# Experts' first layer: a set's four sums kept in PSUM banks instead of SBUF tiles

## The chip, the cores and the metric

One Trainium2 (trn2) chip, one core. The metric is the device time of one execution in microseconds (us). A program's time is the median of its runs.

## What is computed

Three stages follow each other: a causal attention with a decay (4 batches, 8 heads, 576 positions, head size 64), a layer `h*cos(h)` between two matrix products, and the stage that the change touches, a mixture of eight experts over 2304 tokens whose gates come from eight Sinkhorn rounds:

```python
def _moe2_ref(x, w_gate, w1, w2):
    N, D = x.shape                       # 2304, 512
    E = w_gate.shape[1]                  # 8
    logits = x @ w_gate
    logits = logits - logits.max()
    P = np.exp(logits)
    for _ in range(8):
        P /= P.sum(1, keepdims=True) + 1e-09
        P /= P.sum(0, keepdims=True) + 1e-09
        P *= N / E
    out = np.zeros((N, D), dtype=np.float32)
    for e in range(E):
        h = np.maximum(x @ w1[e], 0.0)   # w1[e]: 512 x 1024
        ye = h @ w2[e]                   # w2[e]: 1024 x 512
        out += P[:, e:e + 1] * ye
    return out
```

## The kernel before, in words

The experts run as 48 **blocks**: three groups of 768 tokens (`p`), eight experts (`e`), and two halves of an expert's 1024 hidden units (`hb`). A block has a first layer and a second layer. fp32 operands are held as two fp16 numbers, a high and a low part, and a product of two such operands is three matmuls (`PASSES`).

**First layer** (`first_layer`, called twice a block, for two **sets** `m` of 256 hidden units). A set is a 2x2 block product of 256 hidden units by 768 tokens, done with seven products in place of eight (`PRODUCTS`, products 0 to 6). Each product is six matmuls of 128x384 (`product`, L1203) into a PSUM bank. Products 0, 2, 4 and 6 accumulate in one bank `y`; product 1 has a bank `b` of kind `bq`; products 3 and 5 accumulate in a second bank `q` of kind `bq`. Between products the bank is read while it still grows. From these readings come four sums: c11 (from product 1 and the copy p1 of `y`), c22 (from `y` after product 4 and the copy p5 of `q`), c12 (from `q` after product 5 and the copy u2 of `y`) and c21 (`y` after product 6). A copy is ScalarE's (`copy`, L1230), an addition VectorE's (`add`, L1235), and each writes an SBUF tile `ct` of a ring of twelve. ScalarE then makes the high part of the rectified sum (`relu_split`, L1222, SBUF to SBUF), and VectorE its low part as `max(sum, 0) - high` (L1223). The low part's instruction is called **low** below; it is not issued at once but put in the list `lows` and taken from it by `low()` at fixed places of the order.

```python
            product(p, w, 4, y, False)
            c22 = add(y, p5)
            relu_split(m, 1, 1, c22)
            hook()
            product(p, w, 5, q, False)
            c12 = add(q, u2)
            ...
            product(p, w, 6, y, False)
```

Product 6 writes the bank `y` from which c22 is read, so it waits until VectorE's addition c22 is done. VectorE works its instructions in the order of the program; in a set that order is: c11, low of c11, c22, c12, low of c22, low of c12, and the low of c21 in the next set or at the second layer's start.

**Second layer** (`second_layer`): 72 matmuls of 128x512 (L1279) into banks of kind `a`, six token tiles of 128; VectorE adds each, times its gate, to `acc` (L1308).

**PSUM** has eight banks: three of kind `a`, three of kind `bq`, two of kind `y`. A kind's banks are given out in turn, and a bank is written anew when its last reader is done. Before, a set takes two `bq` banks.

**The weights of the next block** are made while a block runs: ScalarE scales them (L1046) and makes high parts (L1055), GpSimd (POOL) makes the weight sums (L1016 to L1019) and all low parts (L1066, 256 elements at a time, SBUF to SBUF). They are handed out by a plan over the groups of the second layer, but POOL's share runs on into the next first layer: the last of it, `wb`, is eight instructions in a row.

**The gates** (`sinkhorn`) are worked during the first three blocks, a step at a time: `hook()` is called seven times a set and twelve times a second layer, 26 times a block, and at listed counts takes one step. A step's matmul uses a `bq` bank.

Of the kernel before, what the change touches and what calls it, by code (L numbers as in the profile page):

```python
# [23 lines left out]
def kernel(  # L24
# [18 lines left out]
    KD = DM // P  # L43
# [12 lines left out]
    NCH = len(CH)  # L56
# [99 lines left out]
    def at(where, n, fn):  # L156
        where.setdefault(n, []).append(fn)
# [48 lines left out]
    with tc.manual_schedule():  # L206
# [556 lines left out]
        largest = keep.tile([P, KD * NCH], F32, name="largest")  # L763
# [15 lines left out]
        def find_scale(nm, cols, bank):  # L779

            gm, gr, scale, back = small["gm"], small["gr"], scales[nm], backs[nm]
            nc.vector.tensor_reduce(gm, cols, axis=AX.X, op=ALU.max)
            yield
            ps = bank()
            nc.tensor.transpose(ps[0:1, 0:P], gm, ident)
            nc.vector.tensor_reduce(gr[0:1, 0:1], ps[0:1, 0:P], axis=AX.X, op=ALU.max)
            yield
            ps = bank()
            nc.tensor.matmul(ps[:, 0:1], ones[0:1, :], gr[0:1, 0:1], start=True, stop=True)
            nc.vector.tensor_scalar(back, ps[:, 0:1], 2.0**-LIMIT, 2.0**LIMIT, ALU.max, ALU.min)  # L790
            nc.vector.tensor_scalar(back.bitcast(I32), back.bitcast(I32), 0x7F800000, None, ALU.bitwise_and)
            nc.vector.tensor_scalar(
                scale.bitcast(I32), back.bitcast(I32), -1.0, float((254 + TOP) << 23), ALU.mult, ALU.add
            )
            nc.vector.tensor_scalar(back, back, 2.0**-TOP, None, ALU.mult)
            yield
# [46 lines left out]
        def split_x(j, xt):  # L843
            c0, n = CH[j]
            for x in range(KD):
                a = acc[:, x, c0 : c0 + n]
                nc.scalar.copy(xt[:, 0, x, :], a)
                nc.vector.tensor_tensor(xt[:, 1, x, :], a, f32(xt[:, 0, x, :]), ALU.subtract)
                nc.vector.tensor_reduce(
                    largest[:, KD * j + x : KD * j + x + 1], a, axis=AX.X, op=ALU.max, apply_absolute_value=True  # L850
                )
                yield
# [4 lines left out]
        def logits(j, xt, step, bank):  # L857
            n = CH[j][1]
            ps = bank()
            for kk in range(KD):  # L860
                for s in range(2):
                    nc.tensor.matmul(
                        ps[:, 0:n], wg_of[0][:, kk, :], xt[:, s, kk, :], start=kk + s == 0, stop=kk == KD - 1 and s == 1
                    )
            lg = keep.tile([P, 512], F32, tag="dm", name="lg")
            nc.scalar.copy(lg[0:16, 0:n], ps[0:16, 0:n])
            if step is not None:
                at(after_l2, step, lambda: logits2(j, lg, bank))
            return lg

        def logits2(j, lg, bank):
            c0, n = CH[j]
            ps = bank()
            nt = n // P
            for x in range(nt):
                nc.tensor.matmul(
                    ps[:, x * NE : (x + 1) * NE], lg[0:16, x * P : (x + 1) * P], sel, start=True, stop=True
                )
            nc.vector.tensor_copy(
                gate[:, c0 // P : c0 // P + nt, :], ps[:, 0 : nt * NE].rearrange("p (t e) -> p t e", e=NE)  # L880
            )
# [30 lines left out]
        for n in range(len(items) + LAG):  # L912
            if n < len(items):
                ps = ahead.pop(n) if n in ahead else layer1(*items[n])
            for fn in after_l1.pop(n, []):
                fn()
            if n >= LAG:
                b, j, i = items[n - LAG]
# [19 lines left out]
        HN = 384  # L938
# [19 lines left out]
        ctmp = []  # L958
# [13 lines left out]
        XL = xp.tile([P, 2, KD, CH[-1][1]], F32R, name="xl")  # L972
        turn_of = {"ct": 0, "tm": 0, "sg": 0}

        def take(kind, tiles):
            n = turn_of[kind]
            turn_of[kind] = n + 1
            return tiles[n % len(tiles)]
# [155 lines left out]
        def bank(kind, bufs):  # L1134
            return ps_e.tile([P, 512], F32, tag=kind, name=kind, bufs=bufs)


        def rows():
            rs = small["rs"]
            nc.vector.tensor_reduce(rs, gate, axis=AX.X, op=ALU.add)  # L1140
            nc.vector.tensor_scalar(rs, rs, 1e-9, None, ALU.add)
            nc.vector.reciprocal(rs, rs)
            nc.vector.tensor_tensor(gate, gate, rs[:, :, None].to_broadcast([P, NT // P, NE]), ALU.mult)
            nc.vector.tensor_reduce(small["cs"], gate.rearrange("p t e -> p e t"), axis=AX.X, op=ALU.add)

        def sinkhorn():
            yield from split_x(NCH - 1, XL)
            lg = logits(NCH - 1, XL, None, lambda: bank("bq", 3))
            yield
            logits2(NCH - 1, lg, lambda: bank("bq", 3))  # L1150
            nc.vector.tensor_reduce(small["gm"], gate, axis=AX.XY, op=ALU.max)
            yield
            ps = bank("bq", 3)
            nc.tensor.transpose(ps[0:1, 0:P], small["gm"], ident)
            nc.vector.tensor_reduce(small["gr"][0:1, 0:1], ps[0:1, 0:P], axis=AX.X, op=ALU.max, negate=True)
            yield
            ps = bank("bq", 3)
            nc.tensor.matmul(ps[:, 0:1], ones[0:1, :], small["gr"][0:1, 0:1], start=True, stop=True)
            nc.vector.tensor_copy(small["ngm"], ps[:, 0:1])
            nc.scalar.activation(gate, gate, AF.Exp, bias=small["ngm"])  # L1160
            rows()
            yield
            finding = find_scale("x1", largest[:, 2 * KD :], lambda: bank("bq", 3))
            for it in range(8):
                ps = bank("bq", 3)
                nc.tensor.matmul(ps[:, 0:NE], ones, small["cs"], start=True, stop=True)
                cf = small["cf"]
                nc.vector.tensor_scalar(cf, ps[:, 0:NE], 1e-9, None, ALU.add)
                nc.vector.reciprocal(cf, cf)
                nc.vector.scalar_tensor_tensor(  # L1170
                    gate, gate, float(NT) / NE, cf[:, None, :].to_broadcast([P, NT // P, NE]), ALU.mult, ALU.mult
                )
                if it + 1 < 8:
                    rows()
                    next(finding, None)
                else:

                    undo = small["gr"]
                    nc.vector.scalar_tensor_tensor(undo, backs["w1"], 1.0 / RAISE, backs["w2"], ALU.mult, ALU.mult)
                    for p, nm in enumerate(("x0", "x1", "x1")):  # L1180
                        g = gate[:, p * TT : (p + 1) * TT, :]
                        nc.vector.tensor_scalar(g, g, undo, backs[nm], ALU.mult, ALU.mult)
                    gates_ready.append(True)
                yield

        gates_ready = []
        sink = sinkhorn()

        GATE_STEPS = (1, 2, 3, 4, 6, 9, 15, 18, 21, 24, 29, 36, 41, 45, 49, 55, 58)
        slot = [0]  # L1190

        def hook():
            slot[0] += 1
# [31 lines left out]
        def first_layer(p, m):  # L1225
            w = W1T[m]

            def copy(ps):
                c = take("ct", ctmp)
                nc.scalar.activation(c, ps[:, 0:HN], AF.Copy, scale=RAISE)  # L1230
                return c

            def add(ps, other):
                c = take("ct", ctmp)
                nc.vector.scalar_tensor_tensor(c, ps[:, 0:HN], RAISE, other, ALU.mult, ALU.add)  # L1235
                return c

            y = bank("y", 2)
            product(p, w, 0, y, True)
            p1 = copy(y)  # L1240
            hook()
            low()
            b = bank("bq", 3)
            product(p, w, 1, b, True)
            c11 = add(b, p1)
            hook()
            low()
            product(p, w, 2, y, False)
            u2 = copy(y)
            relu_split(m, 0, 0, c11)  # L1250
            hook()
            low()
            q = bank("bq", 3)
            product(p, w, 3, q, True)
            p5 = copy(q)
            hook()
            product(p, w, 4, y, False)
            c22 = add(y, p5)
            relu_split(m, 1, 1, c22)
            hook()  # L1260
            product(p, w, 5, q, False)
            c12 = add(q, u2)
            relu_split(m, 0, 1, c12)
            hook()
            low()
            product(p, w, 6, y, False)
            c21 = copy(y)
            relu_split(m, 1, 0, c21)
            hook()
            low()  # L1270
# [123 lines left out]
```

## Time and profile before

| | |
|---|---|
| median of three runs | 2147.79 us (2146.71 to 2150.45) |
| profiled execution, its time | 2150.18 us |
| its span, first to last instruction | 2148.4 us |
| mean granted TensorE clock | 0.998 |
| busy: ScalarE 63%, POOL 60%, VectorE 58% of the span | |
| share of the chain that ended last: PE 78%, VectorE 10%, ScalarE 5%, issue 4% | |

The profiled execution's own time is 1.8 us more than its span and 2.4 us above the median of the runs. The experts' blocks begin at 670 us and fill the rest. PE is TensorE, DVE VectorE, ACT ScalarE. A matmul's duration overlaps with that of the next one, so a row of six matmuls of 326 ns each takes about 0.97 us from its start to the next product's start.

### The profile page before, as it was taken

To read this page: it belongs to the slowest core of one execution; us is meant where nothing else is said; L and a number is where in the kernel's file an instruction comes from. 1 tells how busy PE (TensorE), PEld (TensorE's weight loads), DVE (VectorE), ACT (ScalarE), POOL (GpSimd) and SP (SyncE) were. 2 spreads that over 40 slices of the span, in tenths; PEclk is the share of its full clock that TensorE was granted. 3 is DMA by queue.
4 is the path that set the end of the run, shared out by engine and by line. 5 is a ranking of instruction groups with operands and counts; after the bars stand their busy time and mean duration, and the time that the engine had idled before them with its cause. 6 is when DMAs were issued, how large, how long until landed. Compare 5 with 4: busy or idle time off the path is not lost.

```text
span 2148.4 us, 34045 instructions
## 1 busy us (share of the span) xinstructions
PE 2061.7 (96%) x12461; PEld 1298.2 (60%) x12461; DVE 1245.3 (58%) x2250; ACT 1351.1 (63%) x2479; POOL 1285.5 (60%) x1794
## 2 busy tenths in 40 slices
PE   8999999999999999999999999999999999999998
PEld 7888988888876544454455444544454445444544
DVE  8999778685656754444455444444555444444444
ACT  7888787777555576555666556556566565556553
POOL 6777455150526576567677675566577755675563
PEclk9999999999999999999999999999999999999999
DMA  5444245353201221122123212221123212212221
GB/s 127 101 106 112 75 163 179 121 177 103 75 1 60 79 75 57 66 79 71 58 69 108 79 60 69 69 79 59 61 78 108 63 66 69 79 59 68 70 79 30
DMA packets 176919, 177.52 MB, mean 83 GB/s; under 512 B 64752, under 2 KB 131696, under 8 KB 176752
## 3 DMA queue, kind: packets, MB, share of 16 engines
q1 hardware_dynamic: 176752, 175.35, 27.1%
q8 instruction: 98, 1.61, 0.3%
q14 instruction: 69, 0.57, 0.1%
HBM read 165.54 MB, written 4.87 MB: 79 GB/s over the span
## 4 chain that ended last, share of the span: by engine, by line
PE 78%; DVE 10%; ACT 5%; issue 4%; POOL 1%; DMA 1%; SPq 0%; POOLq 0%; ACTq 0%; DVEq 0%
PE a L1279 35%; PE y L1203 16%; PE bq L1203 9%; PE ph L175 4%; PE a L822 4%; PE pv L593 2%; PE pst L543 2%; DVE h L1223 2%; PE pss L486 1%; PE pss L487 1%; PE pv L573 1%; DVE ct L1235 1%; PE psq L366 1%; DVE t L196 1%; DVE dm L135 1%
## 5 line engine op out<-in xcount | busy, mean ns | idle before, releaser
L1279 PE MATMUL a<-wb,h 128*128 128x512 f16 x3456 | 754.9, 379 | 0.2 <-ACT acc L1297 0.2
L1203 PEld LDWEIGHTS <-wa 128*128 128x128 f16 x4032 | 394.4, 98 | 332.6 <-issue 69.9
L1279 PEld LDWEIGHTS <-h 128*128 128x128 f16 x3456 | 338.1, 98 | 401.5 <-issue 0.5
L1203 PE MATMUL y<-xc,wa 128*128 128x384 f16 x2304 | 430.9, 327 | 58.1 <-DVE ct L1235 57.9
L1308 DVE SCALAR_TENSOR_TENSOR acc<-a,gate,acc 128x512 f32<-128x512 f32 x264 | 197.4, 750 | 384.9 <-PE a L1279 384.6
L1223 DVE SCALAR_TENSOR_TENSOR h<-ct,h 128x384 f16<-128x384 f32 x384 | 307.1, 811 | 175.8 <-ACT h L1222 164.2
L1016 POOL TENSOR_TENSOR tm<-sg 128x256 f32<-128x256 f32 x96 | 71.2, 742 | 501.7 <-issue 485.8
L1203 PE MATMUL bq<-xc,wa 128*128 128x384 f16 x1728 | 327.9, 326 | 0.7 <-ACT ct L1230 0.7
L1222 ACT ACTIVATE h<-ct 128x384 f16<-128x384 f32 x384 | 197.9, 522 | 204.3 <-DVE ct L1235 201.3
L1230 ACT ACTIVATE ct<-y 128x384 f32<-128x384 f32 x288 | 140.4, 488 | 279.6 <-PE y L1203 279.5
L1066 POOL TENSOR_TENSOR wb<-sg,wb 128x256 f16<-128x256 f32 x384 | 252.4, 697 | 0.0
L1066 POOL TENSOR_TENSOR wa<-tm,wa 128x256 f16<-128x256 f32 x384 | 250.2, 684 | 0.0
L822 PE MATMUL a<-H,w 128*128 128x512 f32 (+1 forms) x960 | 214.3, 371 | 6.0 <-DVE acc L837 3.0
L175 PE MATMUL ph<-xt,w 128*128 128x512 f32 (+1 forms) x960 | 211.6, 369 | 0.9 <-DVE H L203 0.9
L1046 ACT ACTIVATE sg<-sg,sw 128x1024 f32<-128x1024 f32 x188 | 210.1, 1141 | 0.0
L822 PEld LDWEIGHTS a<-H,w 128*128 128x128 f32 x960 | 175.6, 189 | 32.6 <-ACT H L201 2.9
L175 PEld LDWEIGHTS ph<-xt,w 128*128 128x128 f32 x960 | 174.9, 188 | 24.0 <-DVE H L203 1.2
L1066 POOL TENSOR_TENSOR wa<-sg,wa 128x256 f16<-128x256 f32 x288 | 189.3, 686 | 0.0
L1235 DVE SCALAR_TENSOR_TENSOR ct<-bq,ct 128x384 f32<-128x384 f32 x192 | 106.4, 554 | 93.6 <-PE bq L1203 93.4
L1055 ACT CAST wa<-tm 128x1024 f16<-128x1024 f32 x94 | 98.4, 1047 | 97.0 <-POOL tm L1019 97.0
L128 POOL TENSOR_SCALAR w<-dx 128x512 fp32r<-128x512 f32 x32 | 19.9, 622 | 154.0 <-DVE dx L127 149.3
L1055 ACT CAST wb<-sg 128x512 f16<-128x512 f32 x188 | 107.2, 618 | 3.0
(203 smaller groups left out, 2515.5 us busy)
## 6 DMA issues: line engine op xcount, KB each, us to landing
sg<-in_moe_w_dram SPq DMA_DIRECT2D x192, 512.0 KB
seen<-in_moe_w_dram SPq DMA_DIRECT2D x64, 256.0 KB
u<-in_moe_w_dram SPq DMA_DIRECT2D x64, 256.0 KB
stg<-in_moe_w_in_dram SPq DMA_DIRECT2D x16, 512.0 KB
stg<-in_moe_w_out_dram SPq DMA_DIRECT2D x16, 512.0 KB
q<-q SPq DMA_DIRECT2D x30, 160.0 KB
out_dram<-acc SPq DMA_DIRECT2D x18, 256.0 KB
qr<-in_q_dram SPq DMA_DIRECT2D x32, 128.0 KB
```

The costliest lines, as they stand in the source:

```text
L175: nc.tensor.matmul(ps[:, 0:n], w[:, ws, kk * P : (kk + 1) * P], XT[j][:, xs, kk, :], start=first, stop=kk == KD - 1 and (ws, xs) == PASSES ...
L822: nc.tensor.matmul(a_of[b, j][x][:, 0:n], w[:, s1, DM + x * P : DM + (x + 1) * P], H[:, s2, 0:n], start=i == 0 and n_ == 0, stop=end and n ...
L1046: nc.scalar.activation(t, t, AF.Copy, scale=scale)
L1055: nc.scalar.copy(hi, src)
L1066: nc.gpsimd.tensor_tensor(lo[:, y : y + k, z : z + c], src[:, y : y + k, z : z + c], hi[:, y : y + k, z : z + c], ALU.subtract,)
L1203: nc.tensor.matmul(ps[:, 0:HN], w[:, ws, a, k, :], XCS[p % 2][b][:, xs, k, :], start=fresh and n == 0, stop=n == 5, skip_group_check=not f ...
L1222: nc.scalar.activation(hi, src, AF.Relu)
L1223: lows.append(lambda: nc.vector.scalar_tensor_tensor(lo, src, 0.0, hi, ALU.max, ALU.subtract))
L1230: nc.scalar.activation(c, ps[:, 0:HN], AF.Copy, scale=RAISE)
L1235: nc.vector.scalar_tensor_tensor(c, ps[:, 0:HN], RAISE, other, ALU.mult, ALU.add)
L1279: nc.tensor.matmul(ps, H[:, s1, c * P : (c + 1) * P], W2T[e * NHB + hb & 1][:, 2 * m + z, s2, :], start=start and n == 0, stop=stop and n ...
L1308: nc.vector.scalar_tensor_tensor(a, v, g, a, ALU.mult, ALU.add)
```

## The change

The sums stay in PSUM. c11 is written over product 1's bank `b`, c12 over `q`, c21 over `y` (ScalarE copies the bank onto itself with the scale), and c22 goes from `y` to a third `bq` bank, taken for it. High parts and lows read the sum there. p1, u2 and p5 still go to SBUF tiles. A set now takes three `bq` banks, that is all of them. Since the `bq` banks are so used, a gate step that falls into a first layer (the first 14 of a block's 26 counts) takes a bank of kind `a`, and one in a second layer a `bq` bank as before.

```diff
+        def spare():
+            return bank("a" if (slot[0] - 1) % 26 < 14 else "bq", 3)
...
-                ps = bank("bq", 3)
+                ps = spare()
...
-            def copy(ps):
-                c = take("ct", ctmp)
+            def copy(ps, c=None):
+                c = take("ct", ctmp) if c is None else c[:, 0:HN]
                 nc.scalar.activation(c, ps[:, 0:HN], AF.Copy, scale=RAISE)
                 return c
 
-            def add(ps, other):
-                c = take("ct", ctmp)
+            def add(ps, other, c):
+                c = c[:, 0:HN]
                 nc.vector.scalar_tensor_tensor(c, ps[:, 0:HN], RAISE, other, ALU.mult, ALU.add)
                 return c
...
-            c11 = add(b, p1)
+            c11 = add(b, p1, b)
...
-            c22 = add(y, p5)
+            c22 = add(y, p5, bank("bq", 3))
...
-            c12 = add(q, u2)
+            c12 = add(q, u2, q)
...
-            c21 = copy(y)
+            c21 = copy(y, y)
```

No instruction is added, removed or moved on any engine; operands and waits differ. In the changed file the lines are L1208 (products), L1227 (high part), L1228 (low), L1236 (copy), L1241 (addition).

VectorE, the first five instructions of a first layer late in the program (`ct` are SBUF tiles, `bq` and `y` PSUM banks, `h` the high and low parts in SBUF), before:

```order
L1235 SCALAR_TENSOR_TENSOR ct7_8756<-bq_15849,ct6_8755 128x384 [waits PE_49,Activation_49]
L1223 SCALAR_TENSOR_TENSOR h000_8726<-ct7_8756,h000_8726 128x384 [waits Activation_49]
L1235 SCALAR_TENSOR_TENSOR ct10_8759<-y_15841,ct9_8758 128x384 [waits PE_49,Activation_49]
L1235 SCALAR_TENSOR_TENSOR ct11_8760<-bq_15866,ct8_8757 128x384 [waits PE_49]
L1223 SCALAR_TENSOR_TENSOR h011_8729<-ct10_8759,h011_8729 128x384 [waits Activation_49]
```

and with the change:

```order
L1241 SCALAR_TENSOR_TENSOR bq_15903<-bq_15903,ct6_8755 128x384 [waits DVE_49,PE_49,Activation_49]
L1228 SCALAR_TENSOR_TENSOR h000_8726<-bq_15903,h000_8726 128x384 [waits Activation_49]
L1241 SCALAR_TENSOR_TENSOR bq_15934<-y_15895,ct8_8757 128x384 [waits DVE_49,PE_49,Activation_49]
L1241 SCALAR_TENSOR_TENSOR bq_15920<-bq_15920,ct7_8756 128x384 [waits PE_49]
L1228 SCALAR_TENSOR_TENSOR h011_8729<-bq_15934,h011_8729 128x384 [waits Activation_49]
```

The order stays. The low (second row) had two SBUF operands and now has one in PSUM and one in SBUF; c11 and c22 have a third wait, on VectorE itself, for the earlier low that read the bank they write.

TensorE, the last of product 2 and the start of product 3 in a block's second set, before:

```order
L1203 MATMUL y_17959<-xc02_8719,wa1_8749 128x384
L1203 LDWEIGHTS wa1_8749
L1203 MATMUL y_17959<-xc02_8719,wa1_8749 128x384
L1203 LDWEIGHTS wa1_8749
L1203 MATMUL bq_17985<-xc03_8720,wa1_8749 128x384
```

and with the change:

```order
L1208 MATMUL y_17268<-xc02_8719,wa1_8749 128x384
L1208 LDWEIGHTS wa1_8749
L1208 MATMUL y_17268<-xc02_8719,wa1_8749 128x384
L1208 LDWEIGHTS wa1_8749
L1208 MATMUL bq_17294<-xc03_8720,wa1_8749 128x384 [waits DVE_49]
```

Product 3 of the second set now waits for VectorE: its bank is the one in which the first set's c12 lay, until that sum's low has read it.

## Rows read from the trace of the kernel before

**Rows 1.** The page's first part: busy us (share of the span) xinstructions.

```profile
PE 2061.7 (96%) x12461; PEld 1298.2 (60%) x12461; DVE 1245.3 (58%) x2250; ACT 1351.1 (63%) x2479; POOL 1285.5 (60%) x1794
```

**Rows 2.** Waits of the whole span: who waited for whom, us in total, times, longest.

```profile
PE y L1203 <- DVE ct L1235: 57.9, 40, 2.5
```

**Rows 3.** Timeline of one block's TensorE, 1514 to 1548 us: start, duration, instruction [idle before].

```profile
1533.83 1.14 PE L1203 MATMUL y<-xc,wa 128*128 128x384 f16 x6
1534.81 1.14 PE L1203 MATMUL bq<-xc,wa 128*128 128x384 f16 x6
1537.40 2.11 PE L1203 MATMUL y<-xc,wa 128*128 128x384 f16 x12 [1.45 <-DVE ct L1235]
...
1541.29 1.14 PE L1203 MATMUL bq<-xc,wa 128*128 128x384 f16 x6
...
1544.22 1.14 PE L1203 MATMUL y<-xc,wa 128*128 128x384 f16 x6
```

**Rows 4.** The same stretch on VectorE.

```profile
1532.16 0.56 DVE L1235 SCALAR_TENSOR_TENSOR ct<-bq,ct 128x384 f32<-128x384 f32 x1 [1.28 <-PE bq L1203]
1533.99 2.88 DVE L1223 SCALAR_TENSOR_TENSOR h<-ct,h 128x384 f16<-128x384 f32 x1 [1.27 <-ACT h L1222]
1536.80 0.54 DVE L1235 SCALAR_TENSOR_TENSOR ct<-y,ct 128x384 f32<-128x384 f32 x1
...
1537.93 1.03 DVE L1223 SCALAR_TENSOR_TENSOR h<-ct,h 128x384 f16<-128x384 f32 x2
...
1543.51 0.56 DVE L1235 SCALAR_TENSOR_TENSOR ct<-y,ct 128x384 f32<-128x384 f32 x1 [0.53 <-PE y L1203]
```

**Rows 5.** The same stretch on POOL.

```profile
1531.39 5.07 POOL L1066 TENSOR_TENSOR wb<-sg,wb 128x256 f16<-128x256 f32 x8
```

**Rows 6.** By source line, whole span: duration ns min/median/max, first and last start us.

```profile
L1223 DVE SCALAR_TENSOR_TENSOR h<-ct,h x384: 542/559/3973, 676.5 to 2129.7; 128x384 f16<-128x384 f32 x192
L1235 DVE SCALAR_TENSOR_TENSOR ct<-bq,ct x192: 541/558/559, 673.6 to 2127.6; 128x384 f32<-128x384 f32 x192
L1308 DVE SCALAR_TENSOR_TENSOR acc<-a,gate,acc x264: 735/751/753, 757.5 to 2144.1; 128x512 f32<-128x512 f32 x132
```

**Rows 7.** Timeline of another block, 1076 to 1092 us, three engines.

```profile
1077.15 6.02 POOL L1066 TENSOR_TENSOR wb<-sg,wb 128x256 f16<-128x256 f32 x8
...
1078.12 0.74 DVE L1223 SCALAR_TENSOR_TENSOR h<-ct,h 128x384 f16<-128x384 f32 x1 [1.27 <-ACT h L1222]
...
1080.16 2.11 PE L1203 MATMUL y<-xc,wa 128*128 128x384 f16 x12
```

**Rows 8.** The chain that ended last, 660 to 2148 us: second layers' starts and lengths.

```profile
752.26 15.54 PE a L1279 x72
...
1088.12 15.54 PE a L1279 x72
...
1175.69 15.54 PE a L1279 x72
...
1632.93 15.54 PE a L1279 x72
...
1666.49 15.54 PE a L1279 x72
...
2128.56 15.55 PE a L1279 x72
```

**Rows 9.** Window: us, busy us (x) of PE, PEld, DVE, ACT, POOL, then PEclk.

```profile
1656.80:1660.40 3.60, 3.54 (x12) 1.70 (x12) 1.85 (x5) 2.00 (x4) 0.00 (x0) 0.53 1.06 292
```

**Rows 10.** Groups by form, VectorE, 0 to 670 us: busy us, mean ns of one.

```profile
L563 DVE SCALAR_TENSOR_TENSOR A<-pst,A 128x384 f16<-128x384 f32 x64 | 35.6, 556 | 4.3 <-ACT A L555 2.4
...
L200 DVE TENSOR_TENSOR ph<-ph,t 128x384 f32<-128x384 f32 x32 | 18.0, 562 | 6.4 <-ACT t L197 6.3
```

**Rows 11.** Groups by form, ScalarE, 0 to 670 us: busy us, mean ns of one.

```profile
L193 ACT ACTIVATE u<-ph,quarter 128x384 f32<-128x384 f32 x32 | 18.1, 565 | 4.8 <-PE ph L175 4.8
```

**Rows 12.** TensorE's waits in the first three blocks, 666 to 752 us.

```profile
PE y L1203 <- DVE ct L1235: 3.0, 3, 1.3
```

More of the change, by code (lines that the diff above doesn't have):

```diff
@@ L1135, in bank @@
             return ps_e.tile([P, 512], F32, tag=kind, name=kind, bufs=bufs)
+        gates_ready = []
+        slot = [0]
         def rows():
@@ L1144, in rows @@
             nc.vector.tensor_reduce(small["cs"], gate.rearrange("p t e -> p e t"), axis=AX.X, op=ALU.add)
+        def spare():
+            return bank("a" if (slot[0] - 1) % 26 < 14 else "bq", 3)
         def sinkhorn():
             yield from split_x(NCH - 1, XL)
-            lg = logits(NCH - 1, XL, None, lambda: bank("bq", 3))
+            lg = logits(NCH - 1, XL, None, spare)
             yield
-            logits2(NCH - 1, lg, lambda: bank("bq", 3))
+            logits2(NCH - 1, lg, spare)
             nc.vector.tensor_reduce(small["gm"], gate, axis=AX.XY, op=ALU.max)
             yield
-            ps = bank("bq", 3)
+            ps = spare()
             nc.tensor.transpose(ps[0:1, 0:P], small["gm"], ident)
@@ L1156, in sinkhorn @@
             yield
-            ps = bank("bq", 3)
+            ps = spare()
             nc.tensor.matmul(ps[:, 0:1], ones[0:1, :], small["gr"][0:1, 0:1], start=True, stop=True)
@@ L1162, in sinkhorn @@
             yield
-            finding = find_scale("x1", largest[:, 2 * KD :], lambda: bank("bq", 3))
+            finding = find_scale("x1", largest[:, 2 * KD :], spare)
             for it in range(8):
-                ps = bank("bq", 3)
+                ps = spare()
                 nc.tensor.matmul(ps[:, 0:NE], ones, small["cs"], start=True, stop=True)
@@ L1184, in sinkhorn @@
                 yield
-        gates_ready = []
         sink = sinkhorn()
         GATE_STEPS = (1, 2, 3, 4, 6, 9, 15, 18, 21, 24, 29, 36, 41, 45, 49, 55, 58)
-        slot = [0]
         def hook():
```

## The prediction

> **What bounds the kernel.** TensorE is busy for 96% of the span [rows 1], so first the 4% is to be found. The table of waits gives one large entry on it: 57.9 us, in 40 pieces, in which a product into `y` waits for VectorE's addition [rows 2]. That is product 6 waiting for c22. The timeline of one block shows it: product 4 starts at 1533.83, product 5 at 1534.81, and product 6, which would follow 0.97 us later at about 1535.78, starts at 1537.40 [rows 3]. On VectorE c22 starts only at 1536.80, since the low of c11 in front of it runs from 1533.99 to 1536.87, 2.88 us [rows 4]. The same instruction takes 0.56 us by its median; its longest is 3.97 [rows 6].
>
> Why is it long? On POOL the eight `wb` instructions run from 1531.39 to 1536.46 [rows 5], and the low ends 0.41 us after the last of them. In the experts' blocks 37 lows are like it (36 of 2.9 us, one of 3.97), and each ends 0.41 to 0.42 us after such a run. The low has both operands in SBUF, as have POOL's. Other VectorE instructions run through the same stretches at their usual length: c11's addition at 1532.16, inside the `wb` run, took 0.56 [rows 4, 5]. No addition L1235 takes over 0.559, and no L1308 over 0.753 of a median 0.751, though most of those fall into POOL's runs [rows 6]. Both have one operand in PSUM and one in SBUF. So what a row of POOL instructions holds up is a VectorE instruction with two SBUF operands.
>
> It does not always hold it through the run. In the block at 1078 us the low got in between two POOL instructions and took 0.74, the `wb` run became 6.02 us long in place of 5.07, and product 6 started at 1080.16 almost in step [rows 5, 7].
>
> The chain that ended last gives what this costs a block, as the distance between second layers' starts. From 1088.12 to 1175.69 lie three blocks of this undisturbed kind: 29.19 us each. From 1666.49 to 2128.56 lie 15 held ones: 30.80 each. Of the 45 distances from 752.26 to 2128.56, 36 are near 30.80, eight between 29.19 and 29.44, and one, from 1632.93 to 1666.49, is 33.56 [rows 8]. In that last one the low held longest, TensorE waited 2.5 us [rows 2], and the granted clock then stood at 0.53 for 3.6 us, which is the lower level, 1.2 GHz [rows 9].
>
> **The change, part by part.**
>
> *The low reads its sum in PSUM.* It then has the operands of L1235: PSUM, SBUF, output to SBUF. The nearest row with its very types, 128x384, fp16 from PSUM fp32 and an SBUF fp16, is L563 with 556 ns [rows 10]. So 0.56 us, held or not. In the block of rows 3 the low would end at 1534.55, before product 4 is done, and c22 would start with the end of product 4, as in the second set, where it starts at 1543.51 and product 6 follows at 1544.22 without idle time [rows 3, 4]. Every distance becomes 29.19: 1376.30 - 45 x 29.19 = 62.75 us less [rows 8]. The slow clock of the one block goes with its wait and is in that sum. In what follows nothing else holds the lows back, since c22's, c12's and c21's lows change in the same way.
>
> *c22 goes to a PSUM bank.* This is the one place where little room is left. In the second set c22 ends at 1543.51 + 0.56 = 1544.07, product 6 starts at 1544.22 [rows 3, 4], and in the held block TensorE starts 0.06 after c22's end (1536.80 + 0.54 to 1537.40): 0.09 us of room. No row shows VectorE reading one bank and writing another; below, L1235 with its 558 ns median writes SBUF [rows 6], above, L200 reads and writes PSUM in 562 [rows 10]. I take 562, 0.01 more, and nothing on the path. The added wait on VectorE itself names a low of the set before, long done. What exceeds the room would cost 96 sets x the excess: 0.1 us a set is 9.6 us.
>
> *c21 stays in `y`.* ScalarE reads and writes PSUM; the nearest row for that is L193, 565 ns [rows 11], with the low's 0.56 after the high part. All three together are under 2 us, and the second layer needs c21's parts only in its fourth group, 18 of 72 matmuls after its start, 18/72 x 15.54 = 3.9 us [rows 8]. Nothing.
>
> *Three `bq` banks a set.* The one new wait on TensorE is product 3 of the second set, for the low of c12 of the first. In the held block the lows of c22 and c12 ended at 1537.93 + 1.03 = 1538.96 and that product started at 1541.29 [rows 3, 4]: 2.3 us of room, and the lows now come sooner. Nothing.
>
> *The gates' banks.* Seventeen steps in the first three blocks; their waits go with VectorE's gate work, not with a bank. TensorE's three waits there, 3.0 us together [rows 12], stay.
>
> **Sum.** 62.75 us less against the profiled execution, whose span of 2148.4 becomes 2085.7 and whose own time 2150.18 becomes 2087.4. The median of the runs is 2.39 below that execution: 2147.79 - 62.8 = **2085.0**.
>
> **A rule that speaks against it.** The Trainium skill, page "SBUF — State Buffer", section "Who interferes with whom", says that a VectorE instruction with two SBUF inputs and a GpSimd instruction that reads SBUF exclude each other, and that the second one waits until the first finishes. By that a low would wait for one POOL instruction, as at 1078 us, and not for four, as at 1533.99; the trace shows both, and the long kind 37 times. The same section says that an instruction with at most one SBUF input does not contend, with which L1235 and L1308 agree.
>
> **The rivals.**
>
> *The low stays long.* If a POOL instruction can hold a low for 0.64 us at most (5.07 / 8 [rows 5]), the low would end by 1533.99 + 0.64 + 0.56 = 1535.19, c22 by 1535.75, and product 6 would never wait. The 2.88 us must then have another cause, which the change may leave alone, or the operand that stays in SBUF is enough to be held. This is the case in which the change doesn't do what it says: 2147.8. Against it stand 37 ends at the same distance from POOL's, and 288 additions with one SBUF operand of which none is long. Chance 0.05.
>
> *Part of it comes back as a short wait in every set.* If c22 takes 0.1 to 0.3 us more than its room, 96 sets cost 10 to 29 us: 2095 to 2114. For it speaks the room of 0.09; against it the 562 of L200. Chance 0.05.
>
> *Slower.* The same place, priced higher: VectorE's reading of one bank and writing of another, or its way past an extra wait, takes so long that product 6 waits in all 96 sets and not in 37. It decides from 62.8 / 96 = 0.65 us over the room, that is from a c22 of 0.56 + 0.09 + 0.65 = 1.3 us; at 1.5 us the time would be 2085 + 96 x 0.85 = 2167. No row with a PSUM operand comes near. Chance 0.03.
>
> **How the numbers follow.** The forecast has what is left, 0.87, with a range of its own from 2080 to 2092: below, if the first three blocks' 3.0 us go too and the distance comes down by some hundredths; above, if c22 exceeds its room by some hundredths in each set. The range reaches to the nearer half of the second rival, 2080 to 2099. Within 0.2%, about 4 us, is what a measurement of this kernel can't tell from no change. Faster: 0.87 and the second rival's 0.05, 0.92; same: 0.05; slower: 0.03.
>
> **What would show it.** The low L1228 never over about 0.6 us while POOL's `wb` run passes over it; VectorE's busy time for the 384 lows near 384 x 0.56 = 215 us; the wait of `y` for VectorE down from 57.9 to about 3 us, all of it in the first three blocks; second layers 29.2 apart throughout; no low clock. Wrong would be: lows still ending 0.41 after POOL, or a short wait before product 6 in every set, or one before product 3 of the second sets.

## The result and the profile after

The change makes the kernel faster: 2086.78 us, median of four runs (2085.18 to 2087.94), against 2149.12 for the kernel before in the same comparison (four runs, 2146.71 to 2151.0). The ratio is 0.9717, 95% interval 0.9702 to 0.9732. The profiled span fell from 2148.4 to 2086.1 us and the granted clock stands at 0.999. The predicted 2085.0 us is 1.8 below the median. Of that, 0.5 lies in the sum, which gave 2087.4 us for the profiled execution where 2087.94 was measured. The rest, 1.2, is how the executions happened to fall: the profiled one lay 2.4 us above its median before and lies 1.2 above it now.

The page of the kernel after, its first part (busy us, share of the span, instructions; compare [rows 1]) and the shares of its chain by engine:

```profile
PE 2054.4 (98%) x12461; PEld 1298.1 (62%) x12461; DVE 1156.7 (55%) x2250; ACT 1337.5 (64%) x2479; POOL 1277.8 (61%) x1794
...
PE 90%; DVE 6%; ACT 2%; issue 1%; POOL 1%; DMA 0%; SPq 0%; POOLq 0%; ACTq 0%; DVEq 0%
```

As many instructions as before on every engine, and VectorE is busy for 1245.3 - 1156.7 = 88.6 us less. In the chain TensorE's share went from 78% to 90%.

The lows of the kernel after, by source line (duration in ns min/median/max, first and last start in us):

```profile
L1228 DVE SCALAR_TENSOR_TENSOR h<-bq,h x288: 545/558/560, 676.8 to 2066.4; 128x384 f16<-128x384 f32 x144
L1228 DVE SCALAR_TENSOR_TENSOR h<-y,h x96: 557/558/559, 681.3 to 2067.3; 128x384 f16<-128x384 f32 x96
```

The longest of 384 lows is 560 ns, where it was 3973 [rows 6]. POOL's work has not moved out of their way: 68 of the lows start inside a POOL run, as in the block that [rows 3 to 5] showed. The same block of the kernel after, timeline of TensorE, VectorE and POOL (start, duration, instruction [idle before]):

```profile
1501.46 1.14 PE L1208 MATMUL y<-xc,wa 128*128 128x384 f16 x6
1502.44 1.14 PE L1208 MATMUL bq<-xc,wa 128*128 128x384 f16 x6
1503.41 2.11 PE L1208 MATMUL y<-xc,wa 128*128 128x384 f16 x12
...
1499.78 0.57 DVE L1241 SCALAR_TENSOR_TENSOR bq<-bq,ct 128x384 f32<-128x384 f32 x1 [1.26 <-PE bq L1208]
1501.59 0.56 DVE L1228 SCALAR_TENSOR_TENSOR h<-bq,h 128x384 f16<-128x384 f32 x1 [1.25 <-ACT h L1227]
1502.70 0.57 DVE L1241 SCALAR_TENSOR_TENSOR bq<-y,ct 128x384 f32<-128x384 f32 x1 [0.55 <-PE y L1208]
...
1498.97 5.09 POOL L1066 TENSOR_TENSOR wb<-sg,wb 128x256 f16<-128x256 f32 x8
```

The low of c11 starts at 1501.59, inside POOL's `wb` run (1498.97 to 1504.06), and takes 0.56 us where it took 2.88 [rows 4]. VectorE then stands idle for 0.55 us until product 4 (started at 1501.46) is done, does c22, and product 6 starts at 1503.41, 0.97 us after product 5. Before, that distance was 1537.40 - 1534.81 = 2.59 [rows 3].

The chain that ended last of the kernel after, the start of the second layer of the third block, two late ones and the last (start, length; compare [rows 8]):

```profile
752.44 15.54 PE a L1285 x72
...
1920.04 15.54 PE a L1285 x72
1949.48 15.54 PE a L1285 x72
...
2066.24 15.55 PE a L1285 x72
```

The 45 distances are 2066.24 - 752.44 = 1313.80 us, against 1376.30 before: 62.50 less. All are 29.19 but one of 29.44 (1920.04 to 1949.48). So the whole difference of the spans, 62.3 us, lies in the experts' blocks from the third on.

### The profile page after: what moved, and what is told of

The parts are those of the page before. It is cut to its first block, busy times and chain, and to the rows that moved or that the text cites. A ratio compares the mean times of both kernels' runs of the same rounds, so it can differ in the third digit from the quotient of the medians.

```text
span 2086.1 us, 34047 instructions
## 1 busy us (share of the span) xinstructions
PE 2054.4 (98%) x12461; PEld 1298.1 (62%) x12461; DVE 1156.7 (55%) x2250; ACT 1337.5 (64%) x2479; POOL 1277.8 (61%) x1794
## 4 chain that ended last, share of the span: by engine, by line
PE 90%; DVE 6%; ACT 2%; issue 1%; POOL 1%; DMA 0%; SPq 0%; POOLq 0%; ACTq 0%; DVEq 0%
PE a L1285 36%; PE y L1208 18%; PE bq L1208 13%; PE ph L175 6%; PE a L822 6%; PE pv L593 2%; PE pst L543 2%; PE pss L486 2%; PE pss L487 1%; PE pv L573 1%; PE psq L366 1%; DVE acc L837 1%; DVE t L196 1%; DVE xt L848 1%; DVE ph L200 1%
## 5 line engine op out<-in xcount | busy, mean ns | idle before, releaser
L1208 PEld LDWEIGHTS <-wa 128*128 128x128 f16 x4032 | 394.2, 98 | 270.3 <-issue 4.7
L1208 PE MATMUL y<-xc,wa 128*128 128x384 f16 x2304 | 429.3, 326 | 3.2 <-DVE bq L1241 3.0
L1208 PE MATMUL bq<-xc,wa 128*128 128x384 f16 x1728 | 327.9, 326 | 0.6 <-ACT ct L1236 0.6
L1236 ACT ACTIVATE ct<-y 128x384 f32<-128x384 f32 x192 | 94.3, 491 | 272.9 <-PE y L1208 272.9
L1066 POOL TENSOR_TENSOR wb<-sg,wb 128x256 f16<-128x256 f32 x384 | 244.3, 675 | 0.0
L1227 ACT ACTIVATE h<-bq 128x384 f16<-128x384 f32 x288 | 140.7, 489 | 154.8 <-DVE bq L1241 154.7
L1228 DVE SCALAR_TENSOR_TENSOR h<-bq,h 128x384 f16<-128x384 f32 x288 | 159.3, 554 | 124.6 <-ACT h L1227 115.0
L1241 DVE SCALAR_TENSOR_TENSOR bq<-bq,ct 128x384 f32<-128x384 f32 x192 | 108.7, 566 | 109.8 <-PE bq L1208 106.1
```

Of the source, the lines that this page charges most:

```text
L1066: nc.gpsimd.tensor_tensor(lo[:, y : y + k, z : z + c], src[:, y : y + k, z : z + c], hi[:, y : y + k, z : z + c], ALU.subtract,)
L1208: nc.tensor.matmul(ps[:, 0:HN], w[:, ws, a, k, :], XCS[p % 2][b][:, xs, k, :], start=fresh and n == 0, stop=n == 5, skip_group_check=not f ...
L1227: nc.scalar.activation(hi, src, AF.Relu)
L1228: lows.append(lambda: nc.vector.scalar_tensor_tensor(lo, src, 0.0, hi, ALU.max, ALU.subtract))
```

## The experiments

Three theories were put against each other. **Hold to the end of the row**: a low with two SBUF operands waits until POOL's whole row of instructions is done, and only c11's low matters for the time. **One instruction**: it waits for one POOL instruction, and the length has another cause. **Banks**: the gain comes from the other sums, or from the gates' banks.

**Only c11 in PSUM.** From the kernel after:

```diff
-            c22 = add(y, p5, bank("bq", 3))
+            c22 = add(y, p5, take("ct", ctmp))
...
-            c12 = add(q, u2, q)
+            c12 = add(q, u2, take("ct", ctmp))
...
-            c21 = copy(y, y)
+            c21 = copy(y)
```

> Of the changed kernel only c11 stays in PSUM; c22, c12 and c21 go to SBUF tiles again, so their lows read two SBUF operands. Theory (the low of c11 stands ahead of c22 on VectorE, and it alone delays product 6): the other lows may be held behind POOL's wb run in the first set, some at over 1 us, but nothing waits for them; second layers stay 29.2 us apart, 2087 us, ratio to before 0.970 to 0.974. Rival (every low, or ScalarE's shorter high parts, carries a share of the gain): some 2110 to 2140 us.

Measured: 2085.16 us, ratio 0.9721 (0.9707 to 0.9736). By source line, and TensorE's waits for the blocks (us in total, times, longest):

```profile
L1228 DVE SCALAR_TENSOR_TENSOR h<-ct,h x288: 544/558/2054, 676.9 to 2064.7; 128x384 f16<-128x384 f32 x144
L1228 DVE SCALAR_TENSOR_TENSOR h<-bq,h x96: 542/558/558, 674.1 to 2060.6; 128x384 f16<-128x384 f32 x96
...
PE y L1208 <- DVE ct L1241: 3.0, 3, 1.3
```

c11's low, from PSUM (`bq`), is never long. The other three, again from SBUF (`ct`), are held at times: 18 are over 0.6 us, the longest 2.05, and TensorE waits for none of them: its three waits are those of the first blocks, and the second layers start 29.19 us apart but for one distance of 29.44. c11 alone gives the whole gain; the other three sums in PSUM are worth nothing measurable here.

**All but c11.** From the kernel after:

```diff
-            c11 = add(b, p1, b)
+            c11 = add(b, p1, take("ct", ctmp))
```

> The changed kernel with c11 alone in an SBUF tile again; c22, c12, c21 and the gates' banks stay as changed. Theory: the low of c11 is held for 2.9 us in some 37 blocks as before, it ends 0.41 us after POOL's run, TensorE waits about 55 us for c22, 2145 to 2150 us, ratio 0.997 to 1.002. Rival (the other sums carry a share): 2100 to 2140 us.

Measured: 2143.86 us, ratio 0.9991 (0.9981 to 1.0001). Waits and lows:

```profile
PE y L1208 <- DVE bq L1241: 54.7, 40, 2.5
...
L1228 DVE SCALAR_TENSOR_TENSOR h<-bq,h x192: 545/556/559, 677.8 to 2122.4; 128x384 f16<-128x384 f32 x192
L1228 DVE SCALAR_TENSOR_TENSOR h<-ct,h x96: 544/559/3894, 675.1 to 2119.3; 128x384 f16<-128x384 f32 x96
L1228 DVE SCALAR_TENSOR_TENSOR h<-y,h x96: 556/558/559, 679.7 to 2123.3; 128x384 f16<-128x384 f32 x96
```

The forty waits of [rows 2] are back. In one program, the lows that read SBUF reach 3894 ns and those that read PSUM at most 559.

**No `wb` low parts.** From the kernel before, with its sums in SBUF. POOL leaves out the low parts of the second layer's weights from the third block on, so the output lacks them:

```diff
-            for hi, lo, src in parts_of(n):
+            for hi, lo, src in parts_of(n) if ejobs[n][0] == "w1" or n < 8 else ():
```

> The kernel before, with POOL's low parts of the second layer's weights (the wb run of eight instructions) left out from the third block on; its output is then computed with old low parts. The sums stay in SBUF. Theory (POOL's run holds the low): no low over 0.6 us in the first layers from the third block on, second layers 29.2 us apart, 2085 to 2090 us, ratio 0.970 to 0.974. Rival (the 2.9 us have another cause, such as the SBUF tile or ScalarE): lows of 2.9 us stay, 2145 to 2150 us.

Measured: 2084.23 us, ratio 0.9718 (0.9701 to 0.9735). The lows:

```profile
L1223 DVE SCALAR_TENSOR_TENSOR h<-ct,h x384: 543/558/560, 673.8 to 2063.2; 128x384 f16<-128x384 f32 x192
```

With POOL's run gone, two SBUF operands cost nothing: no low over 560 ns, and the blocks are 29.19 us apart but for two of 29.44 and 29.46. So it takes both, POOL's run and the second SBUF operand; either one taken away gives the same gain.

**Finer `wb` pieces.** From the kernel before, 128 elements at a time for `wb` in place of 256, so 16 POOL instructions in place of 8:

```diff
-                k = max(1, PIECE // cols)
-                c = min(cols, PIECE)
+                piece = P if ejobs[n][0] == "w2" else PIECE
+                k = max(1, piece // cols)
+                c = min(cols, piece)
```

> The kernel before, with POOL's wb low parts worked in sixteen instructions of 128 elements in place of eight of 256. Theory (a low that comes while the row of POOL instructions runs back to back waits for the end of the row): the row is some 0.3 to 1.5 us longer, the low of c11 ends 0.41 us after its end and grows to 3.2 to 4.4 us, and the time is 2155 to 2240 us, the upper part if the clock falls after the longer waits. Rival (a low waits for one POOL instruction, whichever comes first has the port until it ends): with instructions of some 0.35 to 0.4 us the low takes at most 1.0 us, product 6 never waits, 2085 to 2090 us.

Measured: 2234.37 us, ratio 1.0418 (1.0402 to 1.0433). Its waits, and the timeline of two blocks on VectorE, POOL and TensorE:

```profile
PE y L1204 <- DVE ct L1236: 101.6, 41, 3.7
```

```profile
1513.81 4.00 DVE L1224 SCALAR_TENSOR_TENSOR h<-ct,h 128x384 f16<-128x384 f32 x1 [1.28 <-ACT h L1223]
...
1511.19 6.21 POOL L1067 TENSOR_TENSOR wb<-sg,wb 128x128 f16<-128x128 f32 x16
...
1518.33 2.11 PE L1204 MATMUL y<-xc,wa 128*128 128x384 f16 x12 [2.57 <-DVE ct L1236]
...
1550.23 3.43 PE L1204 MATMUL y<-xc,wa 128*128 128x384 f16 x12 [2.55 <-DVE ct L1236]
```

POOL's run became 6.21 us long, an instruction in it 6.21 / 16 = 0.39 us. Had the low waited for one instruction, it would have been under a microsecond. It took 4.00 and ended at 1517.81, 0.41 us after POOL's run (1511.19 + 6.21 = 1517.40). Of the lows 38 are so (3.96 to 5.09 us), and each ends 0.41 to 0.42 after a run. For these the row's end sets the end of the low, not the size of an instruction in the row.

The two waits above are equally long, and what follows them is not: twelve matmuls in 2.11 us, then in 3.43. Windows over both (length; busy us and count of PE, PEld, DVE, ACT, POOL; granted clock, DMA share, GB/s):

```profile
1518.30:1520.30 2.00, 1.97 (x13) 1.19 (x13) 1.47 (x3) 1.75 (x4) 0.00 (x0) 1.00 0.82 259
1550.20:1553.40 3.20, 3.17 (x12) 1.59 (x12) 2.02 (x4) 2.00 (x4) 0.00 (x0) 0.60 0.49 164
```

In the second stretch the mean granted clock is 0.60: most of it at the lower of the two levels, 1.2 GHz, which is half of 2.4. Held blocks whose clock stays up lie 31.9 us apart, those whose clock falls 33.6, and these are about two thirds of them. The kernel before showed such a fall once in the experts' blocks, behind a wait of 2.5 us [rows 2, 9]. As an estimate from the distances, 38 x (31.9 - 30.8) = 42 us of the 89 that this run is slower come from the longer hold, and 26 x 1.7 = 44 from the clock behind it. The hold alone would have given some 2190 us, the middle of what was expected; the clock takes the time to the upper end.

**A copy ahead of c22.** From the kernel after, an unused copy of 192 columns of `y` on VectorE, into a tile that nothing reads, to fill the room ahead of product 6:

```diff
-        xp.tile([P, 2 * P], F32, name="gap")
+        spill = xp.tile([P, 2 * P], F32, name="gap")
...
+            nc.vector.tensor_copy(spill[:, 0:192], y[:, 0:192])
             c22 = add(y, p5, bank("bq", 3))
```

> The changed kernel with one more VectorE instruction in each of the 96 sets, a copy of 128x192 elements from the bank y to an unused SBUF tile, right ahead of c22's addition and free to start when the addition was. It should put the addition off by some 0.26 us. Theory (c22 has 0.09 us of room before product 6 waits): each set waits 0.15 to 0.19 us more, 14 to 18 us in all, ratio to before 0.977 to 0.981, and TensorE's wait for c22 shows as some 90 entries. Rival (no room at all): 25 us, ratio about 0.983. Rival (room of 0.3 us or more): no change against the changed kernel, ratio 0.970 to 0.974.

Measured: 2096.14 us, ratio 0.9771 (0.9752 to 0.9791), 9.4 us more than the kernel after and less than the expected 14 to 18. Timeline of one set on VectorE and TensorE, then the waits:

```profile
1507.03 0.36 DVE L1264 COPY gap<-y 128x192 f32<-128x192 f32 x1 [0.49 <-PE y L1208]
1507.30 0.56 DVE L1241 SCALAR_TENSOR_TENSOR bq<-y,ct 128x384 f32<-128x384 f32 x1
...
1505.85 1.14 PE L1208 MATMUL y<-xc,wa 128*128 128x384 f16 x6
1506.83 1.14 PE L1208 MATMUL bq<-xc,wa 128*128 128x384 f16 x6
1507.91 2.11 PE L1208 MATMUL y<-xc,wa 128*128 128x384 f16 x12
```

```profile
PE y L1208 <- DVE bq L1241: 4.1, 4, 1.6
```

c22 starts 1507.30 - 1505.85 = 1.45 us after product 4, against 1502.70 - 1501.46 = 1.24 in the kernel after (product 4 starts there at 1501.46): 0.21 later. Product 6 follows product 5 after 1.08 us in place of 0.97, so about half of the 0.21 is lost, and the other half, some 0.11, was room. Two sets of 0.105 lost make 0.21: the blocks lie 29.40 us apart in place of 29.19. A loss of 0.15 to 0.19 a set was expected, from a copy that puts c22 off by 0.26 and a room of 0.09. The table of waits was expected to show some 90 new entries and shows one more. Product 5's modelled end, 1506.83 + 1.14 = 1507.97, lies behind product 6's start at 1507.91, so no idle time is there to be listed. A wait of this size shows in the distances alone.

**The gates' banks.** From the kernel after, the gate steps take a `bq` bank again:

```diff
-            return bank("a" if (slot[0] - 1) % 26 < 14 else "bq", 3)
+            return bank("bq", 3)
```

> The changed kernel with all gate steps on bq banks as before, though a set now takes all three of them. Theory (the gates' banks cost nothing either way: seventeen steps in three blocks, each bank read within a microsecond): within 2 us of the changed kernel, ratio 0.970 to 0.974. Rival (a set has to wait for a bank that a gate step holds, or a gate step for a set's sum): up to seven first-layer steps of some 2 us each, 2090 to 2100 us, ratio 0.974 to 0.979, and waits of products into bq for VectorE in the first three blocks.

Measured: 2086.16 us, ratio 0.9729 (0.971 to 0.9749), the same as with the change. Two of its waits:

```profile
PE y L1208 <- DVE bq L1241: 2.9, 3, 1.3
...
PE bq L862 <- DVE h L1228: 0.3, 1, 0.3
```

One new wait of 0.3 us; the moved gates are worth nothing either way.

**The low behind c22.** Another cure, in the kernel before: the call of c11's low is moved from ahead of product 2 to behind c22, so that VectorE does c22 first.

```diff
             hook()
-            low()
             q = bank("bq", 3)
...
             c22 = add(y, p5)
+            low()
             relu_split(m, 1, 1, c22)
```

> The kernel before, sums in SBUF, with the low of c11 moved behind c22's addition in VectorE's order, one place. Theory (the held low costs only because c22 is queued behind it): c22 starts with the end of product 4, the low is still held, for some 1.5 us up to 0.41 us after POOL's row, c12 is late behind it and nothing on TensorE waits for c12; second layers 29.2 us apart, ratio 0.970 to 0.974. Rival (the held low costs through something else, c12 or the high parts behind it): a wait of TensorE of 1 us or more stays in some 37 blocks, ratio above 0.985.

Measured: 2108.2 us, ratio 0.9832 (0.9816 to 0.9848): a gain of 37 us, where the theory expected about 60. TensorE's waits in the blocks, then the timeline on VectorE, ScalarE and TensorE:

```profile
PE y L1203 <- ACT ct L1230: 16.5, 37, 1.5
```

```profile
1512.98 0.56 DVE L1235 SCALAR_TENSOR_TENSOR ct<-y,ct 128x384 f32<-128x384 f32 x1 [2.37 <-PE y L1203]
1513.46 1.32 DVE L1223 SCALAR_TENSOR_TENSOR h<-ct,h 128x384 f16<-128x384 f32 x1
1514.70 0.55 DVE L1235 SCALAR_TENSOR_TENSOR ct<-bq,ct 128x384 f32<-128x384 f32 x1
...
1515.28 0.52 ACT L1222 ACTIVATE h<-ct 128x384 f16<-128x384 f32 x1 [1.18 <-DVE ct L1235]
...
1516.64 0.47 ACT L1230 ACTIVATE ct<-y 128x384 f32<-128x384 f32 x1
...
1515.63 1.14 PE L1203 MATMUL bq<-xc,wa 128*128 128x384 f16 x6
1517.16 1.14 PE L1203 MATMUL y<-xc,wa 128*128 128x384 f16 x6 [0.40 <-ACT ct L1230]
```

c22 (1512.98) is now in time and product 6 waits no more. But the low behind it is held for 1.32 us, c12 comes after it at 1514.70, its high part on ScalarE at 1515.28, and behind that on ScalarE stand c21's two instructions and the copy p1 of the second set (1516.64). Product 2 of the second set writes the bank that this copy reads: it starts 1.53 us after product 1 in place of 0.97. Most of the held blocks are 29.72 to 29.77 us long; two, in which the low took 2.4 us, are 30.84 and 30.86. That nothing on TensorE waits for c12 was wrong: through ScalarE, product 2 of the next set does. Here the moved hold found another waiter; the one that the change removes finds none.

## Why the prediction was right

- **The low, 0.56 us, held or not.** Right: 558 ns median, 560 at most, and 159.3 + 53.6 = 212.9 us for all of them by their two groups, where 215 was expected. The reason, too, stood: held lows are found only in the runs that keep a low with two SBUF operands beside POOL's `wb` run, and there only among the lows that read SBUF.
- **The sum, 62.75 us.** 62.50 in the 45 distances, 62.3 in the span. The missing 0.25 was counted wrongly. The prediction took every distance to become 29.19, also the one of 29.44, in which the low took 0.74 [rows 7]. One of 29.44 remains after, with no long low anywhere. The chain there:

```profile
1947.29 0.04 DVEq L1241
1947.33 0.40 issue
1947.72 0.58 DVE bq L1241
1948.30 0.04 issue
1948.34 1.14 PE y L1208 x6
```

  c22 starts 0.40 us late with nothing to wait for that the profile shows. The chain of the kernel before has the same in its distance of 29.44 (1058.68 to 1088.12):

```profile
1079.16 0.40 issue
1079.55 0.57 DVE ct L1235
```

  The block at 1564.79, whose low took 0.74 too, has 29.19. So the 0.25 was not the low's, and a change to the lows couldn't take it away; what the 0.40 is stays open. Another 0.18 us is that the second layer of the third block starts at 752.44 and not at 752.26 [rows 8].
- **c22 in a bank, 562 ns, room 0.09.** 567 by the median; the copy ahead of c22 puts the room at 0.11. The rival of a short wait in every set did not come, and that run prices it: about 1 us of the total for each 0.01 us a set.
- **c21 in `y`, nothing.** Right, and the bound of 565 was high: ScalarE's copy of the bank onto itself took 484 ns on average. High parts read PSUM a little faster, too. ScalarE's groups after, by form (busy us, mean ns | idle before, releaser):

```profile
L1227 ACT ACTIVATE h<-bq 128x384 f16<-128x384 f32 x288 | 140.7, 489 | 154.8 <-DVE bq L1241 154.7
...
L1236 ACT ACTIVATE y<-y 128x384 f32<-128x384 f32 x96 | 46.5, 484 | 0.8 <-PE y L1208 0.7
```

- **Three `bq` banks, the gates' banks, the first blocks' 3.0 us.** Right. TensorE's waits from 660 to 750 us follow; from 745 us to the end the profile lists none.

```profile
PE y L1208 <- DVE bq L1241: 3.0, 3, 1.3
PE bq L1208 <- ACT ct L1236: 0.6, 1, 0.6
...
```

- **The rival "the low stays long"** rested on one POOL instruction being all that can hold a low. The finer pieces refute that for the 38 held lows of that run. The Trainium skill, page "SBUF — State Buffer", section "Who interferes with whom", says that a VectorE instruction with at most one SBUF input, outside the modes that use both port pairs, doesn't contend with GpSimd: for the lows the traces agree (560 ns at most). The same page of the Trainium skill, section "SBUF: two separate sides", says that of a VectorE instruction with two SBUF inputs and a GpSimd instruction that reads SBUF, the one that starts first has the shared ports for its whole instruction, and the other blocks. By that, 0.39 us of waiting was the most that a low could meet among the finer pieces; 4.00 was measured, and the measurement decides.

**What stays open** is when a low gets in. Some get in after one POOL instruction, as at 1078 us in [rows 7]; most of c11's lows are held to the row's end. (The run there is 6.02 us long not for that low alone: three more got in before its end, and three POOL instructions took 0.99 in place of 0.67.) Where in a POOL instruction the low arrives doesn't tell the two apart: in the kernel before, the low at 1165.94 came 0.25 us into one and took 0.84, and that at 1652.36 came 0.26 us into one and took 3.97, through six. Nine blocks follow a second layer in which VectorE has, besides the lows, instructions with all their operands in SBUF. In eight of them c11's low gets in, and in no other; but the ninth is the block at 1652.36, with the longest hold of all. Whether those instructions are the cause was not tried.

## What to carry to other kernels

Where a VectorE instruction shows a normal median and a maximum several times longer, look at what GpSimd does at its end: if it ends a fixed time after a run of GpSimd instructions and has two SBUF operands, leave one operand in PSUM, and begin with the held instruction that delays one for which another engine waits. Here cutting GpSimd's pieces finer made it worse (ratio 1.0418), and moving the instruction gave 37 us in place of 62, since something else then waited behind it. After such a cure look for the next small wait in the distances between equal stages, since a wait shorter than a matmul's modelled tail was in no table of waits here (0.105 us a set, 9.4 us in all).

## What the runs showed of the hardware

- A VectorE instruction with two SBUF operands can wait for a whole row of POOL instructions that follow each other: 2.88 us through four of them, 3.97 through six, up to 5.09 among the finer pieces, ending 0.41 to 0.42 us after the row each time. In other blocks the same instruction got in after one or two of them, in 0.67 to 1.11 us.
- POOL gains as well when the lows read only one operand in SBUF: a `wb` instruction takes 675 ns on average, 697 before.
- With 384 columns of fp32, VectorE's addition takes 567 ns into PSUM and 558 into SBUF (medians); ScalarE's high part takes 489 from PSUM and 522 from SBUF (means).
- Two waits of TensorE of about 2.5 us each, 32 us apart in one program, were followed by a granted clock of 1.00 once and of 0.60 the other time; the runs don't show what decides it.
